# Attention with normalised q and k, then a SiLU feed-forward: squares on ScalarE, softmax sums on VectorE alone, weight rounding later and split one piece ahead

## The chip, the cores and the metric

The kernel runs on one core of one Trainium2 chip. The metric is the device time of one execution, in microseconds (us). Five queues work at once and meet only through semaphores: TensorE (PE; its weight loads are PEld), VectorE (DVE), ScalarE (ACT), GpSimd (POOL) and SyncE (SP), which here issues nearly all transfers. Each runs its own instructions strictly in order.

## What is computed

Eight batches, 12 heads, 448 positions, head size 64. Every row of q and k is divided by its root mean square and scaled by a gain; then softmax attention; then a feed-forward block of 768 -> 2048 -> 768 with SiLU over all 3584 rows.

```python
def rmsnorm(x, g):
    rms = np.sqrt(np.mean(x * x, axis=-1, keepdims=True) + 1e-06)
    return x / rms * g
scores = scale * np.matmul(q_n, k_n.transpose(0, 1, 3, 2))
attn = np.exp(scores - np.max(scores, axis=-1, keepdims=True))
attn = attn / (np.sum(attn, axis=-1, keepdims=True) + 1e-09)
x = np.matmul(attn, v)          # heads side by side: 3584 x 768
h = x @ w_in                    # 768 x 2048
return ((h * (1.0 / (1.0 + np.exp(-h)))) @ w_out).astype(np.float32)
```

The activations arrive as float32; the two weight matrices arrive as float64, and the kernel rounds them to float32 itself.

## The kernel before

**Pairs.** The work is cut into 48 *pairs*: one batch and two neighbouring heads (six pairs a batch, numbered 0 to 47 here). A row of 448 positions is folded into 112 partitions x 4 columns (`j`). For each pair the function `bounded` does: `normalise` (squares `sq`, sums per row `rms`, a power of -1/2, and the scaled rows `qn` and `kn`), `transpose` of q and of k through TensorE into `qT` and `kT`, `scores` (in two halves of two `j` each, TensorE, then the exponential `e` on ScalarE), `weigh` (`e` times `v`, into `av`), `add_up` (the softmax denominators: the sum `es` of the four `e`), `unload` (ScalarE copies `av` out as `xU`), and `divide` (a matmul with ones spreads the sums over partitions, VectorE takes the reciprocal `r` and multiplies, giving `xT`). `divide` of pair n stands inside pair n+1; `normalise` is two pairs ahead.

**Feed-forward as filler.** From pair 6 on, the feed-forward of the batch before is cut into pieces of single matmuls, and `fill()`, called four times in each pair, issues an equal share of them between the attention steps. Each block of six matmuls (`h`, line 386) is turned into `g_own` and `g_joint` by SiLU on ScalarE; the `mm` buffers that hold `h` are two, so TensorE can be one block ahead of ScalarE and no more. The second product (line 402) is evacuated by VectorE into `o` and stored. Batch 0 has no filler: its six pairs, called the *startup* below, run attention alone.

**Weights.** `w_in` comes in 24 pieces of 128 x 512, `w_out` in 32 pieces of 128 x 384. `round` makes float32 of a float64 piece: two ScalarE instructions read the low and the high words (lines 119 and 120, into `last` and into the weight itself), three VectorE instructions build the rounded bits (lines 121, 124, 128), and one GpSimd add (line 132) finishes. For `w_in` there are ten places for raw pieces and four for `last`; for `w_out` two for `last` and three for raw, the latter shared with the output tiles `o`. How many pieces are rounded in each quarter of a pair is written out by hand:

```python
rounds = [1, 0, 1, 0] if b == 0 else [3, 3, 3, 3]
```

so twelve pieces are rounded in the startup and the other 44 in pairs 6 to 9, here called the *weights stage*. Loads of raw pieces stand in SP's queue, up to ten pieces ahead, among the loads of q, k and v for two pairs ahead.

The whole order is the order of the code (manual schedule). The steps named in the prediction are at lines 274 to 292 (normalise), 306 and 308 (`qT`, `kT`), 346 and 351 (`es`), 356 (`xU`), 365 to 371 (divide), 119 to 132 (a round), 435 (the list above).

Of the kernel before, what the change touches and what calls it, by code (L numbers as in the profile page):

```python
# [46 lines left out]
class Weights:  # L47
# [7 lines left out]
    def __init__(self, nc, pool, w_in, w_out, z):  # L55
# [15 lines left out]
        self.pieces += [  # L71
            (self.W2[:, f, ts(half, z.HALF)], w_out[ts(f, P), ts(half, z.HALF)])
            for f in range(z.NF)
            for half in range(2)
        ]
        self.raws = []
        self.rounded = 0

    def load(self):
        i = len(self.raws)  # L80
        if i == len(self.pieces):
            return
        dst, src = self.pieces[i]
        raw = None
        if src.dtype == I64:
            if i < self.n_in:
                raw = self.stage[i % self.NRAW]
            else:
                raw = self.raw_pool.tile([128, 2 * dst.shape[-1]], I32, name="raw", tag="o")
            self.nc.sync.dma_start(raw.bitcast(I64), src)  # L90
        else:
            self.nc.sync.dma_start(dst, src)
        self.raws.append(raw)

    def round(self, ahead):
# [7 lines left out]
        if i == len(self.pieces):  # L103
            return
        while len(self.raws) <= i:
            self.load()
        self.rounded += 1
        if self.raws[i] is not None:
            nc = self.nc
            w = self.pieces[i][0]  # L110
            n = w.shape[-1]
            wi = w.bitcast(I32)
            words = self.raws[i].rearrange("p (n two) -> p n two", two=2)
            low, high = words[:, :, 0], words[:, :, 1]
            if i < self.n_in:
                last = self.low[i % 4]
            else:
                last = self.raw_pool.tile([128, n], I32, name="last", tag="last", bufs=2)
            nc.scalar.activation(last, low.bitcast(U32), AF.Copy, scale=2.0**-29)
            nc.scalar.activation(w, high.bitcast(F32), AF.Abs)  # L120
            nc.vector.tensor_scalar(  # L121
# [9 lines left out]
            )  # L131
            nc.gpsimd.tensor_tensor(out=wi, in0=wi, in1=last, op=ALU.add)  # L132
        while len(self.raws) < min(i + 1 + ahead, len(self.pieces)):

            if len(self.raws) >= self.n_in and self.rounded < self.n_in:
                break
            self.load()


@with_exitstack  # L140
def kernel(
# [21 lines left out]
    nc = tc.nc  # L163
# [58 lines left out]
    def arm():  # L222

        own = [dict(st) for st in state]
        w = copy.copy(weights)
        w.raws = list(weights.raws)
        return dict(
# [25 lines left out]
def bounded(  # L253
# [6 lines left out]
    mp = ctx.enter_context(tc.tile_pool(name="mp", bufs=1))  # L260
    op = weights.raw_pool = ctx.enter_context(tc.tile_pool(name="op", bufs=3))
    ps = ctx.enter_context(tc.tile_pool(name="ps", bufs=1, space=bass.MemoryType.PSUM))
# [3 lines left out]
    def normalise(n):  # L266
# [5 lines left out]
        for i, name in enumerate("qk"):  # L272
            sq = at.tile([R, 2, J, D], F32, name="sq")
            nc.gpsimd.tensor_tensor(out=sq, in0=st[name], in1=st[name], op=ALU.mult)  # L274
            nc.vector.tensor_reduce(out=rms[:, i], in_=sq, axis=AX.X, op=ALU.add)  # L275
        flat = rms.rearrange("p i h j -> p (i h j)")
# [6 lines left out]
        for i, name in enumerate("qk"):  # L283
            rows = at.tile([R, J, 2, D], F32, name=name + "n")
            st[name + "n"] = rows
            factor = rms[:, i].rearrange("p h (j one) -> p h j one", one=1)
            nc.gpsimd.tensor_tensor(
                out=rows.rearrange("p j h d -> p h j d"),
                in0=st[name],
                in1=factor.to_broadcast([R, 2, J, D]),  # L290
                op=ALU.mult,
            )

    def transpose(n, name):
# [10 lines left out]
        if name == "q":  # L305
            nc.vector.tensor_copy(dst, t)  # L306
        else:
            nc.vector.tensor_scalar_mul(out=dst, in0=t, scalar1=gains)  # L308
# [29 lines left out]
    def add_up(n, half):  # L338

        st = state[n]  # L340
        if half == 0:
            st["es"] = [at.tile([R, S], F32, name="es", bufs=2) for _ in range(2)]
        for h, eng in ((0, nc.vector), (1, nc.gpsimd)):
            es = st["es"][h]
            if half == 0:
                eng.tensor_tensor(  # L346
                    out=es, in0=st["e", 0][:, h, :], in1=st["e", 1][:, h, :], op=ALU.add
                )
            else:
                for j in (2, 3):  # L350
                    eng.tensor_tensor(out=es, in0=es, in1=st["e", j][:, h, :], op=ALU.add)  # L351

    def unload(n):
        st = state[n]
        st["xU"] = at.tile([P, S], F32, name="xU", bufs=2)
        nc.scalar.copy(st["xU"], st["av"])  # L356

    def divide(n):
# [5 lines left out]
        for h in range(2):  # L364
            nc.tensor.matmul(  # L365
                t[ds(h * D, D), :], ones[0:R, :], st["es"][h], start=True, stop=True
            )
# [9 lines left out]
    def feed_forward(b):  # L377
# [282 lines left out]
```

## Time and profile before

| | |
|---|---|
| median of 3 runs | 1708.61 us (1708.14 to 1709.46) |
| the profiled execution | 1709.11 us, span of its instructions 1707.3 us |
| PE busy | 1609.5 us, 94% of the span; mean granted clock 0.973 |
| DVE, ACT, POOL busy | 577.3, 438.9 and 583.5 us (34%, 26%, 34%) |
| transfers | 70.23 MB, 41 GB/s over the span |

The span is cut by what TensorE does: up to the first scores at 18.93 us loads and the first normalisation; then the startup, six pairs up to 124.9 us; then the weights stage, until about 300 us; then, until the last division at 1546.8 us, attention and feed-forward interleaved; then the last batch's feed-forward alone. "Granted clock" is the share of TensorE's full 2.4 GHz that it was allowed; half of that (1.2 GHz) is the other level, so a mean between 0.5 and 1 is a mixture. A row's idle time is that of its engine just before it, and the name behind the arrow is what ended it.

### The profile page before, as it was taken

Reading aid. Unit: us, or ns where it says so; the run is one execution under the profiler, and the core shown is the slowest. Engines: PE = TensorE matmul, PEld = TensorE weight load, DVE = VectorE, ACT = ScalarE, POOL = GpSimd, SP = SyncE. Lnnn points to the kernel's source line nnn. Section 1 sums busy time; section 2 is a strip of 40 time slices with the busy share of each in tenths; the row PEclk is TensorE's granted clock in tenths of the full one; section 3 lists DMA queues with packets and bytes.
Section 4 is the critical chain, followed back from the end, with each engine's and each line's share of the span. In section 5 each row is a group of like instructions: output and inputs, shape, how many; then the busy total and the mean of one; then the engine's idle time right before and its main releaser. Section 6 shows DMA issues by size and latency. Waiting matters only on the chain.

```text
span 1707.3 us, 14310 instructions
## 1 busy us (share of the span) xinstructions
PE 1609.5 (94%) x5440; PEld 792.0 (46%) x5440; DVE 577.3 (34%) x708; ACT 438.9 (26%) x696; POOL 583.5 (34%) x448
## 2 busy tenths in 40 slices
PE   4668688999999999999999999999999999999998
PEld 1223234544455444544455444554455544455555
DVE  4778766232223323232222322333222322230000
ACT  2335354123311143123311134203310133310100
POOL 6776545333323333342232333333323333310000
PEclk9878888999999999999999999999999999999999
DMA  6331343110011100110001100011001100000000
GB/s 212 94 101 62 100 126 90 51 42 17 17 31 31 42 27 6 46 41 22 17 26 31 46 17 17 26 47 32 17 11 33 54 28 17 10 10 9 1 19 20
DMA packets 51985, 70.23 MB, mean 41 GB/s; under 512 B 5316, under 2 KB 44740, under 8 KB 51908
## 3 DMA queue, kind: packets, MB, share of 16 engines
q1 hardware_dynamic: 51584, 69.23, 14.0%
q8 instruction: 45, 0.74, 0.2%
q14 instruction: 32, 0.26, 0.0%
q10 hardware_dynamic: 324, 0.00, 0.0%
HBM read 58.20 MB, written 11.01 MB: 41 GB/s over the span
## 4 chain that ended last, share of the span: by engine, by line
PE 87%; DVE 8%; POOL 2%; ACT 2%; issue 1%; DMA 0%; SPq 0%; POOLq 0%; ACTq 0%; DVEq 0%
PE mm L402 35%; PE mm L386 32%; PE sc L316 9%; PE av L330 7%; PE tr L365 2%; PE tr L302 2%; DVE W L124 1%; DVE W L128 1%; DVE es L351 1%; DVE r L369 1%; DVE W L121 1%; POOL rms L280 1%; DVE es L346 0%; POOL sq L274 0%; POOL W L132 0%
## 5 line engine op out<-in xcount | busy, mean ns | idle before, releaser
L386 PE MATMUL mm<-xT,W 128*128 128x448 f32 x1536 | 606.4, 549 | 38.1 <-ACT g_joint L394 31.7
L402 PE MATMUL mm<-W,g_own 128*128 128x384 f32 x1536 | 512.7, 489 | 0.0
L386 PEld LDWEIGHTS mm<-xT,W 128*128 128x128 f32 x1536 | 286.4, 191 | 340.2 <-issue 296.1
L402 PEld LDWEIGHTS mm<-W,g_own 128*128 128x128 f32 x1536 | 286.5, 190 | 217.9 <-issue 32.0
L321 ACT ACTIVATE e<-sc 112x896 f32<-112x896 f32 x192 | 166.5, 914 | 505.9 <-PE sc L316 395.2
L369 DVE RECIPROCAL r<-tr 128x448 f32<-128x448 f32 x48 | 141.9, 2956 | 285.8 <-PE tr L365 285.8
L274 POOL TENSOR_TENSOR sq<-k 112x512 f32<-112x512 f32 x48 | 49.9, 1039 | 468.3 <-DVE rms L275 468.3
L316 PE MATMUL sc<-qT,kT 64*112 64x448 f32 x768 | 182.1, 595 | 24.4 <-DVE kT L308 24.4
L330 PE MATMUL av<-e,v 112*64 112x448 f32 x768 | 168.6, 561 | 0.9 <-ACT e L321 0.9
L351 POOL TENSOR_TENSOR es<-es,e 112x448 f32<-112x448 f32 x96 | 128.0, 1333 | 88.9 <-ACT e L321 84.7
L280 POOL TENSOR_TENSOR rms<-rms,minus_half 112x16 f32<-112x16 f32 x48 | 139.7, 2910 | 48.4 <-DVE rms L277 48.4
L408 DVE COPY o<-mm 128x384 f32<-128x384 f32 x56 | 31.2, 557 | 341.9 <-PE mm L402 341.9
L346 POOL TENSOR_TENSOR es<-e 112x448 f32<-112x448 f32 x48 | 56.6, 1180 | 252.2 <-PE tr L365 249.1
L394 ACT ACTIVATE g_own<-mm 128x384 f32<-128x384 f32 x128 | 62.6, 489 | 280.3 <-PE mm L386 279.5
L316 PEld LDWEIGHTS sc<-qT,kT 64*112 64x112 f32 x768 | 64.6, 183 | 127.3 <-issue 85.8
L308 DVE TENSOR_SCALAR kT<-tr,gains 128x448 f32<-128x448 f32 x48 | 32.7, 682 | 197.9 <-PE tr L302 197.9
L275 DVE TENSOR_REDUCE rms<-sq 112x8 f32<-112x512 f32 x96 | 65.4, 682 | 73.9 <-POOL sq L274 73.9
L330 PEld LDWEIGHTS av<-e,v 112*64 112x64 f32 x768 | 52.2, 141 | 81.1 <-issue 66.5
L356 ACT COPY xU<-av 128x448 f32<-128x448 f32 x48 | 25.5, 532 | 237.2 <-PE av L330 237.0
L306 DVE COPY qT<-tr 128x448 f32<-128x448 f32 x48 | 29.8, 622 | 167.3 <-PE tr L302 167.3
L402 PE MATMUL mm<-W,g_joint 128*128 128x384 f32 x256 | 85.6, 490 | 0.0
L321 ACT ACT_TABLE_LOAD x44 | 56.5, 1283 | 106.0 <-PE sc L316 58.8
(38 smaller groups left out, 868.6 us busy)
## 6 DMA issues: line engine op xcount, KB each, us to landing
W<-in_moe_w_in_dram SPq DMA_DIRECT2D x24, 512.0 KB, 4.2
raw<-in_moe_w_out_dram SPq DMA_DIRECT2D x32, 384.0 KB, 3.3
q<-in_q_dram SPq DMA_DIRECT2D x48, 224.0 KB, 3.1
k<-in_k_dram SPq DMA_DIRECT2D x48, 224.0 KB, 3.6
v<-in_v_dram SPq DMA_DIRECT2D x48, 224.0 KB, 3.3
out_dram<-o SPq DMA_DIRECT2D x16, 168.0 KB, 2.1
out_dram<-o SPq DMA_DIRECT2D x16, 144.0 KB, 2.0
out_dram<-o SPq DMA_DIRECT2D x16, 120.0 KB, 2.0
```

What stands on the lines that cost most here:

```text
L274: nc.gpsimd.tensor_tensor(out=sq, in0=st[name], in1=st[name], op=ALU.mult)
L275: nc.vector.tensor_reduce(out=rms[:, i], in_=sq, axis=AX.X, op=ALU.add)
L280: nc.gpsimd.tensor_tensor(out=flat, in0=flat, in1=minus_half[0:R].to_broadcast([R, 4 * J]), op=ALU.pow)
L316: nc.tensor.matmul(banks[:, h, 0:S], st["kT"][r, ts(j, R)], st["qT"][r, :], start=True, stop=True,)
L321: nc.scalar.activation(st["e", j], banks[:, :, 0:S], AF.Exp)
L330: nc.tensor.matmul(st["av"][ds(h * D, D), :], st["v"][:, h, j, :], st["e", j][:, h, :], start=(j == 0), stop=(j == J - 1),)
L346: eng.tensor_tensor(out=es, in0=st["e", 0][:, h, :], in1=st["e", 1][:, h, :], op=ALU.add)
L351: eng.tensor_tensor(out=es, in0=es, in1=st["e", j][:, h, :], op=ALU.add)
L369: nc.vector.reciprocal(out=r, in_=t)
L386: nc.tensor.matmul(h, W1[:, c, ts(f, P)], xT[b][c], start=(c == 0), stop=(c == z.NW - 1))
L394: nc.scalar.activation(dst, h[:, cols], AF.Silu)
L402: nc.tensor.matmul(t, g[:, f, :], W2[:, f, ts(half, z.HALF)], start=(f == 0), stop=(f == z.NF - 1),)
```

## The change

1. **Squares.** `sq` on GpSimd and its buffer are gone. ScalarE writes the squares into the tiles `qn` and `kn`, which `normalise` later overwrites with the scaled rows; VectorE sums from there. So a square now waits until the transposes of the pair before have read those tiles.
2. **`qT`** is copied out by ScalarE instead of VectorE.
3. **`es`** is one tile for both heads, added by VectorE in three instructions of 112 x 896; before, VectorE did one head and GpSimd the other, three instructions of 112 x 448 each. `es` and `xU` now have one buffer per use, `o` two.
4. **Rounding** is cut in two: `split` issues the two ScalarE instructions, `round` the rest, and `round` ends by splitting the next piece. The counts per quarter become `[0, 0, 0, 1]` and `[2, 3, 2, 3]`: six pieces in the startup, 50 in pairs 6 to 10. Raw pieces of `w_out` have three buffers of their own.
5. **`w_out` by halves.** Its pieces are ordered first by column half, and the second product does all row tiles of one half before the other.

```diff
         self.pieces += [
             (self.W2[:, f, ts(half, z.HALF)], w_out[ts(f, P), ts(half, z.HALF)])
+            for half in range(2)
             for f in range(z.NF)
-            for half in range(2)
         ]
+        self.lasts = []
...
-                raw = self.raw_pool.tile([128, 2 * dst.shape[-1]], I32, name="raw", tag="o")
+                raw = self.raw_pool.tile([128, 2 * dst.shape[-1]], I32, name="raw", tag="raw", bufs=3)
...
+    def split(self):
+        i = len(self.lasts)
+        if i == len(self.pieces):
+            return
+        while len(self.raws) <= i:
+            self.load()
+        last = None
+        if self.raws[i] is not None:
+            w = self.pieces[i][0]
+            words = self.raws[i].rearrange("p (n two) -> p n two", two=2)
+            if i < self.n_in:
+                last = self.low[i % len(self.low)]
+            else:
+                last = self.raw_pool.tile([128, w.shape[-1]], I32, name="last", tag="last", bufs=2)
+            self.nc.scalar.activation(last, words[:, :, 0].bitcast(U32), AF.Copy, scale=2.0**-29)
+            self.nc.scalar.activation(w, words[:, :, 1].bitcast(F32), AF.Abs)
+        self.lasts.append(last)
...
-        while len(self.raws) <= i:
-            self.load()
+        while len(self.lasts) <= i:
+            self.split()
...
-            nc.scalar.activation(last, low.bitcast(U32), AF.Copy, scale=2.0**-29)
-            nc.scalar.activation(w, high.bitcast(F32), AF.Abs)
...
-            nc.gpsimd.tensor_tensor(out=wi, in0=wi, in1=last, op=ALU.add)
+            nc.gpsimd.tensor_tensor(out=wi, in0=wi, in1=self.lasts[i], op=ALU.add)
...
+        if len(self.lasts) < len(self.raws) and len(self.lasts) == self.rounded:
+            self.split()
...
-            sq = at.tile([R, 2, J, D], F32, name="sq")
-            nc.gpsimd.tensor_tensor(out=sq, in0=st[name], in1=st[name], op=ALU.mult)
-            nc.vector.tensor_reduce(out=rms[:, i], in_=sq, axis=AX.X, op=ALU.add)
+            rows = at.tile([R, J, 2, D], F32, name=name + "n")
+            st[name + "n"] = rows
+            by_head = rows.rearrange("p j h d -> p h j d")
+            nc.scalar.activation(by_head, st[name], AF.Square)
+            nc.vector.tensor_reduce(out=rms[:, i], in_=by_head, axis=AX.X, op=ALU.add)
...
-            nc.vector.tensor_copy(dst, t)
+            nc.scalar.copy(dst, t)
...
-        for h, eng in ((0, nc.vector), (1, nc.gpsimd)):
-            es = st["es"][h]
-            if half == 0:
-                eng.tensor_tensor(
-                    out=es, in0=st["e", 0][:, h, :], in1=st["e", 1][:, h, :], op=ALU.add
+            st["es"] = at.tile([R, 2, S], F32, name="es")
+            nc.vector.tensor_tensor(
+                out=st["es"], in0=st["e", 0], in1=st["e", 1], op=ALU.add
+            )
+        else:
+            for j in (2, 3):
+                nc.vector.tensor_tensor(
+                    out=st["es"], in0=st["es"], in1=st["e", j], op=ALU.add
...
-        for g, c0 in tiles:
-            for half in range(2):
+        for half in range(2):
+            for g, c0 in tiles:
...
-        rounds = [1, 0, 1, 0] if b == 0 else [3, 3, 3, 3]
+        rounds = [0, 0, 0, 1] if b == 0 else [2, 3, 2, 3]
```

**How the order moves, first place: VectorE in one startup pair.** VectorE's queue in the startup repeats from pair to pair. Before, one repetition reads (`W_81` is `w_in`'s float32 tile, `W_82` the room in which its raw pieces lie):

```order
L121 TENSOR_SCALAR W_81<-W_81 128x512
L124 TENSOR_SCALAR W_81<-W_81 128x512
L128 SCALAR_TENSOR_TENSOR W_81<-W_82,W_81 128x512
L369 RECIPROCAL r<-tr 128x448
L371 TENSOR_TENSOR xT<-xU,r 128x448
L346 TENSOR_TENSOR es<-e 112x448
L306 COPY qT<-tr 128x448
L351 TENSOR_TENSOR es<-es,e 112x448 x2
L121 TENSOR_SCALAR W_81<-W_81 128x512
L124 TENSOR_SCALAR W_81<-W_81 128x512
L128 SCALAR_TENSOR_TENSOR W_81<-W_82,W_81 128x512
L308 TENSOR_SCALAR kT<-tr,gains 128x448
```

Now the same stretch of VectorE's queue, from one `kT` to the next, reads:

```order
L323 TENSOR_SCALAR kT<-tr,gains 128x448
L292 TENSOR_REDUCE rms<-qn 112x8
L292 TENSOR_REDUCE rms<-kn 112x8
L294 TENSOR_SCALAR rms<-rms 112x16
L134 TENSOR_SCALAR W_81<-W_81 128x512
L137 TENSOR_SCALAR W_81<-W_81 128x512
L141 SCALAR_TENSOR_TENSOR W_81<-W_82,W_81 128x512
L383 RECIPROCAL r<-tr 128x448
L385 TENSOR_TENSOR xT<-xU,r 128x448
L358 TENSOR_TENSOR es<-e 112x896
L363 TENSOR_TENSOR es<-es,e 112x896 x2
```

The round between the last `es` and `kT` is gone, `qT` is gone, and the `es` additions are twice as wide.

**Second place: ScalarE in one startup pair.** Before, ScalarE's queue from one pair's second half to the next pair's reads:

```order
L321 ACTIVATE e<-sc 112x896 x2
L356 COPY xU<-av 128x448
L119 ACTIVATE W_82<-W_82 128x512
L120 ACTIVATE W_81<-W_82 128x512
L321 ACTIVATE e<-sc 112x896 x2
L119 ACTIVATE W_82<-W_82 128x512
L120 ACTIVATE W_81<-W_82 128x512
```

Now one repetition of it reads:

```order
L336 ACTIVATE e<-sc 112x896 x4
L321 COPY qT<-tr 128x448
L370 COPY xU<-av 128x448
L291 ACTIVATE qn<-q_58 112x2x4x64
L291 ACTIVATE kn<-k_60 112x2x4x64
L112 ACTIVATE W_82<-W_82 128x512
L113 ACTIVATE W_81<-W_82 128x512
```

The four exponentials of a pair stand together, and the copy, the two squares and the one split stand between them and the next pair's.

**Third place: ScalarE in the weights stage, at the end of pair 8.** Before, the end of a pair in that stage (pair 7) reads on ScalarE (`last` and `raw` are numbered buffers of `w_out`'s pieces, `W2_82` its float32 tile):

```order
L119 ACTIVATE last_1109<-raw_904 128x384
L120 ACTIVATE W2_82<-raw_904 128x384
L119 ACTIVATE last_1118<-raw_937 128x384
L120 ACTIVATE W2_82<-raw_937 128x384
L119 ACTIVATE last_1127<-raw_946 128x384
L120 ACTIVATE W2_82<-raw_946 128x384
L394 ACTIVATE g_own_788<-mm_1083 128x384
L394 ACTIVATE g_joint_789<-mm_1083 128x64
L394 ACTIVATE g_own_788<-mm_1139 128x384
L394 ACTIVATE g_joint_789<-mm_1139 128x64
L321 ACT_TABLE_LOAD
```

Now ScalarE's queue at the end of pair 8 reads:

```order
L291 ACTIVATE qn_1166<-q0_58 112x2x4x64
L291 ACTIVATE kn_1169<-k0_60 112x2x4x64
L112 ACTIVATE last_1182<-raw_983 128x384
L113 ACTIVATE W2_82<-raw_983 128x384
L112 ACTIVATE last_1191<-raw_992 128x384
L113 ACTIVATE W2_82<-raw_992 128x384
L112 ACTIVATE last_1200<-raw_1028 128x384
L113 ACTIVATE W2_82<-raw_1028 128x384
L408 ACTIVATE g_own_703<-mm_1151 128x384
L408 ACTIVATE g_joint_704<-mm_1151 128x64
L408 ACTIVATE g_own_703<-mm_1205 128x384
L408 ACTIVATE g_joint_704<-mm_1205 128x64
```

The two squares now stand ahead of the splits, and the splits are those of one piece later; the SiLU instructions still stand behind all of them. In SP's queue the loads of q, k and v stand behind up to twelve loads of raw `w_out` pieces, before and after.

## Rows read from the trace of the kernel before

**Rows 1.** busy time by stage: us, busy (x instructions) per engine, granted clock, DMA share, GB/s

```profile
18.93:124.90 105.97, 68.73 (x261) 24.29 (x261) 79.21 (x94) 39.22 (x55) 81.24 (x59) 0.81 0.36 107
124.90:300.00 175.10, 137.03 (x418) 62.20 (x420) 124.21 (x176) 86.81 (x154) 96.30 (x80) 0.86 0.34 97
300.00:1546.80 1246.80, 1246.80 (x4309) 619.35 (x4306) 361.72 (x419) 303.15 (x455) 397.07 (x297) 1.00 0.10 28
```

**Rows 2.** timeline of VectorE, four divisions: start, us, engine, line, operation, idle before

```profile
139.06 2.95 DVE L369 RECIPROCAL r<-tr 128x448 f32<-128x448 f32 x1
...
366.53 2.96 DVE L369 RECIPROCAL r<-tr 128x448 f32<-128x448 f32 x1 [2.07 <-PE tr L365]
...
573.98 2.96 DVE L369 RECIPROCAL r<-tr 128x448 f32<-128x448 f32 x1 [2.07 <-PE tr L365]
...
760.78 2.96 DVE L369 RECIPROCAL r<-tr 128x448 f32<-128x448 f32 x1 [2.07 <-PE tr L365]
```

**Rows 3.** chain of waits over one startup pair: start, us, what

```profile
71.12 3.35 PE sc L316 x8
...
74.63 0.92 ACT e L321
...
77.61 0.69 DVE W L128
78.30 2.88 DVE r L369
...
81.20 1.25 DVE xT L371
...
85.51 1.36 DVE es L351
...
88.39 0.61 DVE kT L308
89.05 3.35 PE sc L316 x8
```

**Rows 4.** instructions by line and shape: busy us, mean ns, idle before

```profile
L356 ACT COPY xU<-av 128x448 f32<-128x448 f32 x48 | 25.5, 532 | 237.2 <-PE av L330 237.0
...
L280 POOL TENSOR_TENSOR rms<-rms,minus_half 112x16 f32<-112x16 f32 x48 | 139.7, 2910 | 48.4 <-DVE rms L277 48.4
...
L275 DVE TENSOR_REDUCE rms<-sq 112x8 f32<-112x512 f32 x96 | 65.4, 682 | 73.9 <-POOL sq L274 73.9
```

**Rows 5.** timeline, six instructions with VectorE beside GpSimd or alone

```profile
44.79 1.26 POOL L132 TENSOR_TENSOR W<-W,W 128x512 int32<-128x512 int32 x1
...
45.33 1.21 DVE L371 TENSOR_TENSOR xT<-xU,r 128x448 f32<-128x448 f32 x1
...
76.69 0.43 DVE L121 TENSOR_SCALAR W<-W 128x512 f32<-128x512 f32 x1 [1.05 <-ACT W L120]
...
78.15 1.76 PE L316 MATMUL sc<-qT,kT 64*112 64x448 f32 x8
...
142.04 0.63 DVE L371 TENSOR_TENSOR xT<-xU,r 128x448 f32<-128x448 f32 x1
...
142.59 0.62 DVE L346 TENSOR_TENSOR es<-e 112x448 f32<-112x448 f32 x1
```

**Rows 6.** timeline around one stall of TensorE in the weights stage

```profile
202.31 0.42 SPq L183 DMA_DIRECT2D q<-in_q_dram  x1
...
202.67 0.55 PE L302 MATMUL tr<-ident,kn 112*128 112x112 f32 x4
...
207.25 1.04 POOL L274 TENSOR_TENSOR sq<-q 112x512 f32<-112x512 f32 x1
...
216.15 1.94 POOL L132 TENSOR_TENSOR W<-W,last 128x384 int32<-128x384 int32 x2
...
217.17 0.55 ACT L119 ACTIVATE last<-raw 128x384 int32<-128x384 uint32 x1 [6.96 <-POOL W L132]
...
218.69 1.11 PE L386 MATMUL mm<-xT,W 128*128 128x448 f32 x1 [9.33 <-ACT g_joint L394]
```

More of the change, by code (lines that the diff above doesn't have):

```diff
@@ L110, in round @@
             w = self.pieces[i][0]
-            n = w.shape[-1]
             wi = w.bitcast(I32)
[L113 to L118, printed above, removed]
-            nc.scalar.activation(last, low.bitcast(U32), AF.Copy, scale=2.0**-29)
-            nc.scalar.activation(w, high.bitcast(F32), AF.Abs)
+            high = self.raws[i].rearrange("p (n two) -> p n two", two=2)[:, :, 1]
             nc.vector.tensor_scalar(
@@ L225, in arm @@
         w = copy.copy(weights)
-        w.raws = list(weights.raws)
+        w.raws, w.lasts = list(weights.raws), list(weights.lasts)
         return dict(
@@ L260, in bounded @@
     mp = ctx.enter_context(tc.tile_pool(name="mp", bufs=1))
-    op = weights.raw_pool = ctx.enter_context(tc.tile_pool(name="op", bufs=3))
+    op = weights.raw_pool = ctx.enter_context(tc.tile_pool(name="op", bufs=2))
     ps = ctx.enter_context(tc.tile_pool(name="ps", bufs=1, space=bass.MemoryType.PSUM))
@@ L283, in normalise @@
         for i, name in enumerate("qk"):
-            rows = at.tile([R, J, 2, D], F32, name=name + "n")
-            st[name + "n"] = rows
             factor = rms[:, i].rearrange("p h (j one) -> p h j one", one=1)
             nc.gpsimd.tensor_tensor(
-                out=rows.rearrange("p j h d -> p h j d"),
+                out=st[name + "n"].rearrange("p j h d -> p h j d"),
                 in0=st[name],
@@ L341, in add_up @@
         if half == 0:
-            st["es"] = [at.tile([R, S], F32, name="es", bufs=2) for _ in range(2)]
-        for h, eng in ((0, nc.vector), (1, nc.gpsimd)):
-            es = st["es"][h]
-            if half == 0:
-                eng.tensor_tensor(
-                    out=es, in0=st["e", 0][:, h, :], in1=st["e", 1][:, h, :], op=ALU.add
-                )
-            else:
-                for j in (2, 3):
-                    eng.tensor_tensor(out=es, in0=es, in1=st["e", j][:, h, :], op=ALU.add)
+            st["es"] = at.tile([R, 2, S], F32, name="es")
[6 more added lines that the diff above has]
+                    out=st["es"], in0=st["es"], in1=st["e", j], op=ALU.add
+                )
     def unload(n):
         st = state[n]
-        st["xU"] = at.tile([P, S], F32, name="xU", bufs=2)
+        st["xU"] = at.tile([P, S], F32, name="xU")
         nc.scalar.copy(st["xU"], st["av"])
@@ L365, in divide @@
             nc.tensor.matmul(
-                t[ds(h * D, D), :], ones[0:R, :], st["es"][h], start=True, stop=True
+                t[ds(h * D, D), :], ones[0:R, :], st["es"][:, h, :], start=True, stop=True
             )
```

## The prediction

> **What bounds the kernel now.** I read the busy times by stage first. The reader is to see three stages [rows 1]: in the startup (18.93 to 124.90 us) TensorE is busy 68.73 of 105.97 us at a mean granted clock of 0.81; in the weights stage (to 300) 137.03 of 175.10 at 0.86; after that 1246.80 of 1246.80 at 1.00. So nothing outside the first 300 us can be gained except at the very end, which the change does not touch. The second view is the timeline of VectorE's divisions, used as a ruler [rows 2]. From the division of pair 5 to that of pair 11, the feed-forward of batch 0 passes: 366.53 - 139.06 = 227.47 us. The same work for batch 2, with no weights to round, takes 760.78 - 573.98 = 186.80. The weights stage thus wastes 40.7 us, idle time and half-clock time together. Third, the chain of waits over one startup pair [rows 3]: scores at 71.12, the next pair's at 89.05, period 17.93 us, and nearly all of it runs through VectorE: a round, `r`, `xT`, `es`, a round, `kT`. Last, a timeline around one TensorE stall in the weights stage [rows 6]: 9.33 us idle, because SiLU stood on ScalarE behind `last`, `last` behind a GpSimd add, and that add behind the whole normalisation on GpSimd (`sq` at 207.25, the add at 216.15).
>
> **The startup after the change.** I replay VectorE's queue from one `kT` to the next, time 0 at `kT`'s end.
> - Two sums of squares at 0.68 and the small factor at 0.17 [rows 4], the latter an estimate from its place between them and the round: to 1.6. The squares come from ScalarE, right after `xU`; a square is 512 elements, the copy of 448 costs 0.53 [rows 4], so I take 0.6.
> - One round, 1.6 (from 76.69 to `r` at 78.30 [rows 3, 5]): to 3.2. Its two ScalarE instructions were issued a pair earlier.
> - `r`, 2.9 [rows 3]: to 6.1. TensorE's divide is there in time: scores take 1.76 at full clock and 3.35 at half [rows 3, 5], and the divide about 1.1 more.
> - Meanwhile GpSimd: the power starts at about 1.9 and takes 2.91 [rows 4], `qn` and `kn` 1.04 each (the shape of `sq` [rows 6]), the add 1.26 [rows 5]: to 8.2.
> - `xT` is ready to go at 6.1, but the trace shows that it will not run: with GpSimd's add at 44.79 to 46.05 beside it, `xT` took 1.21 and ended 0.5 after the add; alone it takes 0.63 [rows 5]. So it ends at 8.7.
> - `es`: 448 elements take 0.62 alone [rows 5] and 1.36 beside GpSimd [rows 3]; GpSimd has nothing left in this part of the pair. For 896 I take 1.1, three times: to 12.0. (Bounds for one: 1.0, and 2.7 if blocked as in rows 3.)
> - `kT` 0.6: 12.6 us, against 17.93.
>
> The Trainium skill, SBUF — State Buffer, "Who interferes with whom", says that an instruction of VectorE with two SBUF inputs and one of GpSimd exclude each other for their whole length. The rows agree (1.21 against 0.63); without that rule the pair would come to 11.2.
>
> What hides the rest: the exponentials, transposes and `qT` (now on ScalarE, 0.53 as for `xU`) lie beside VectorE. ScalarE's four exponentials at 0.92, two copies, two squares and one split (1.1: the exponential ends at 75.55, VectorE's round starts at 76.69 [rows 3, 5]) sum to 7.0 of 12.6. The new wait is the square of k, which needs the transposes of k; behind it stand the split and the next pair's exponentials. It costs the first exponential about 0.9, and `xT`'s wait for GpSimd covers that.
>
> Sum: six pairs took 105.97, so the first took 105.97 - 5 x 17.93 = 16.3. After: the first, without divide and rounds, 11; five of 12.6; 1.3 for the one pair with two splits before its exponentials: 75.3. The exponentials' table is now loaded for the squares, ahead of need, and the first scores come 0.4 earlier. Scores of pair 6 then start near 93.8. Pair 5's division stood 14.2 after them; now two rounds instead of three are ahead of it, the second delayed by GpSimd until 9.5, so 11. It moves from 139.06 to 104.8: gain 34.3.
>
> **The weights stage after the change.** 50 rounds in five pairs instead of 44 in less than four. A round takes VectorE about 1.9 there (124.21 busy [rows 1], less some 10 of its own for each of four pairs, over 44 rounds; 1.6 is the bound below), so ten rounds and the 10 are 29 of the 31.1 that TensorE needs for a pair (186.80 / 6); GpSimd loses `sq` and `es`. So no engine is the bound, but waits in ScalarE's queue are.
> - Pair 6: TensorE reaches the matmul that needs pair 5's `xT` at 11.2 after the scores, and has it at 14.7: 3.5, with 1.5 for the half clock behind it: 5.
> - Pairs 7 and 8, last quarter: the third `last` has to wait for the add two pieces before, and that add stands behind the normalisation on GpSimd, as today. Counted from the end of the transposes of k (203.2 in rows 6): square and sum 1.5, factor and start 0.5, power 2.9, two multiplies 2.1, two adds 2.2, one split 1.1, SiLU 0.7, semaphores 0.6: 11.6. TensorE has 6.1 of work meanwhile (203.2 to 218.69 - 9.33 = 209.36), so it idles 5.5 where it idled 9.33. Half clock afterwards adds 2.5 (scores 3.35 for 1.76 and a few matmuls). 8 each: 16.
> - Pairs 9 and 10 have no SiLU behind the splits; only the next exponentials come late, under a quarter of filler: 2 in all.
>
> Waste 23 instead of 40.7: gain 17.7.
>
> **At nothing.** `w_out` by halves changes no matmul and no store's size; the first half is rounded before it is needed. Two `o` buffers instead of three still let one be filled while the other is stored. From 300 us on, ScalarE is busy 303 of 1247 us [rows 1]; two squares and a copy a pair add 1.73 x 37 = 64, hidden under TensorE's continuous work, and 64 is the price if none of it were.
>
> **Sum.** The profiled execution took 1709.1 (span 1707.3 and 1.8 around it). 1709.1 - 34.3 - 17.7 = 1657.1. The median of the runs is 0.5 below that execution: 1656.6. Own range 1645 to 1672.
>
> **Rivals.**
> - *The clock stays low in the startup.* For: mean 0.81 there, and the scores ran at 3.35, half speed, after every wait for `kT` [rows 1, 3]. Then scores, `weigh` and transposes at half clock make TensorE the loop: 16 a pair. Against: TensorE idles 6.2 us a pair now (105.97 less 68.73, over six) and would idle 1 to 3. Loss against mine 5 x 3.4 = 17: 1674. The Trainium skill, TensorE: Matmul & The Clock Gate, "Part 1: The HAM clock gate (the "warmup" mystery)", says that the throttled state is the default and activity releases it; by that a loop with TensorE busy three quarters of the time should do better than now, but no run here shows it.
> - *Waste goes with the pairs that round.* 40.7 over 3.67 pairs is 11.1 a pair; five pairs make 55.5. For: the same chain `last`, add, power stands there. Against: GpSimd has 2 x 1.04 less in it, and the stall's length is 6.1 less than the chain's. 1709.1 - 34.3 + 14.8 - 0.5 = 1689.
> - *No stall is left:* the early split takes SiLU off the chain, waste 5: 1639.
> - *Slower: q arrives late and ScalarE stands for it.* In SP's queue q for two pairs ahead stands behind up to twelve raw pieces that wait for rounds; at 202.31 it was issued only 4.9 before its use on GpSimd [rows 6]. Now its reader is ScalarE, with SiLU and all exponentials behind it. Lateness adds one for one to the stall. With 5 more than today's per pair, 16 to 19 in five pairs make 80 to 95: the startup gain of 34.3 is gone from 15 a pair upward (75 = 40.7 + 34.3). At 19: 1709.1 - 34.3 + 54.3 - 0.5 = 1729. Against: raws are loaded three deep, and 6.1 us of filler follow the round that frees the last of them.
> - *The startup doesn't shorten,* because GpSimd's power and the squares' path (square, sum, power, two multiplies: 8 in a row) set its pace: 1709.1 - 17.7 - 0.5 = 1691; with the waste unchanged too, 1709, no change.
>
> **How the numbers follow.** Mine 0.56; low clock 0.14; waste with pairs 0.12; no stall 0.09; slower 0.05; startup not shorter 0.04. Range 1638 to 1689 holds all but about 0.15. A measurement here tells about 0.2%, 3.4 us, from no change: faster 0.92, same 0.03, slower 0.05.
>
> **What would show it.** Startup scores 12 to 13 apart in place of 17.93, `es` of 112 x 896 near 1.1, `xT` near 2 or waiting for GpSimd, pair 5's division near 105; from there to pair 11's about 210 instead of 227; two idles of TensorE of 5 to 6 us ended by SiLU, in pairs 7 and 8; nothing idle after pair 11. I am wrong if the startup's period stays above 15, if squares wait for q's transfer, or if any wait of TensorE shows up after 350 us.

## The result and the profile after

The changed kernel takes 1668.22 us (median of 4 runs, 1666.87 to 1669.05) against 1708.38 (1708.07 to 1709.46): ratio 0.9763, 95% interval 0.9746 to 0.978. The forecast was 1656.6 with a range of 1638 to 1689: the direction was right and the time lay in the range, but 11.6 us of the forecast gain of 52 did not come. The profiled execution has a span of 1666.6 us and a mean granted clock of 0.986.

The busy times by stage answer to [rows 1]; the columns are the same.

```profile
18.43:110.00 91.57, 73.99 (x310) 27.66 (x311) 78.84 (x90) 52.23 (x80) 48.85 (x31) 0.91 0.43 122
110.00:300.00 190.00, 162.37 (x518) 76.68 (x518) 125.17 (x184) 95.15 (x169) 79.52 (x62) 0.92 0.36 103
...
350.00:1500.00 1150.00, 1150.00 (x3965) 570.29 (x3964) 327.20 (x349) 342.93 (x533) 165.41 (x102) 1.00 0.10 27
```

TensorE is still continuously busy from 350 us on, though ScalarE does two squares and a copy more in each pair. All of the difference lies before that. The ruler of VectorE's divisions ([rows 2]) says where; here are the divisions of pairs 5 to 11.

```profile
100.61 2.94 DVE L383 RECIPROCAL r<-tr 128x448 f32<-128x448 f32 x1
...
134.69 2.96 DVE L383 RECIPROCAL r<-tr 128x448 f32<-128x448 f32 x1 [0.51 <-PE tr L379]
...
175.79 2.96 DVE L383 RECIPROCAL r<-tr 128x448 f32<-128x448 f32 x1 [3.86 <-PE tr L379]
...
220.34 2.96 DVE L383 RECIPROCAL r<-tr 128x448 f32<-128x448 f32 x1 [3.79 <-PE tr L379]
...
257.42 2.95 DVE L383 RECIPROCAL r<-tr 128x448 f32<-128x448 f32 x1
...
299.75 2.96 DVE L383 RECIPROCAL r<-tr 128x448 f32<-128x448 f32 x1 [5.54 <-PE tr L379]
...
325.79 2.96 DVE L383 RECIPROCAL r<-tr 128x448 f32<-128x448 f32 x1 [2.05 <-PE tr L379]
```

Pair 5's division moved from 139.06 to 100.61: 38.45 us, where 34.3 were forecast. From there to pair 11's it takes 225.18 instead of 227.47: a gain of 2.29, where 17.7 were forecast. The two make 40.7, the whole of the difference between the profiled executions (spans 1707.3 and 1666.6). So the startup paid more than forecast, and the weights stage next to nothing. Cut at the first scores of pair 6 instead (124.90 before, 93.8 forecast, 90.87 after), the gains are 34.0 and 6.7 us where 31.1 and 20.9 were forecast: the sizes depend on the cut, the finding does not.

The ruler can be read pair by pair. Each interval between two divisions, less the interval of the same two pairs in batch 2 (32.88, 32.12, 32.12, 31.61, 32.04 and 26.04, 186.81 together), is the waste of that pair in us. In pair 6 the ruler shows less than was lost when pair 5's division comes late, since TensorE has then worked ahead of it:

| pair | 6 | 7 | 8 | 9 | 10 | 11 | sum |
|---|---|---|---|---|---|---|---|
| before | 13.5 | 13.7 | 13.6 | -0.1 | 0.0 | 0.0 | 40.7 |
| forecast | 5 | 8 | 8 | 2 for both | | 0 | 23 |
| after | 1.2 | 9.0 | 12.4 | 5.5 | 10.3 | 0.0 | 38.4 |

What TensorE waited for in that stage, as a table of its waits (engine and line waited for: us in total, times, longest):

```profile
PE mm L400 <- ACT g_joint L408: 18.4, 3, 9.9
PE mm L416 <- POOL W L145: 6.9, 2, 6.3
PE mm L400 <- DVE xT L385: 3.7, 1, 3.7
PE mm L416 <- DVE o L422: 2.3, 1, 2.3
```

And ScalarE's own waits there, from the same view:

```profile
ACT last L112 <- POOL W L145: 40.6, 11, 8.3
...
ACT qn L291 <- DMA q<-in_q_dram: 14.3, 3, 6.1
```

The first line is the chain that the prediction named: `last` behind GpSimd's adds, and these behind the normalisation. The second is the wait that it held unlikely: a square waits for the transfer of q, three times. The timeline of pair 8 shows both, ending in TensorE's longest stall (start, us, engine, line, operation, idle before):

```profile
181.73 10.63 SPq L91 DMA_DIRECT2D raw<-in_moe_w_out_dram  x5
...
192.41 0.42 SPq L198 DMA_DIRECT2D q<-in_q_dram  x1
...
192.49 0.55 PE L317 MATMUL tr<-ident,kn 112*128 112x112 f32 x4
...
196.37 0.63 ACT L291 ACTIVATE qn<-q 112x512 f32<-112x512 f32 x1 [3.68 <-DMA q<-in_q_dram]
...
198.95 2.94 POOL L297 TENSOR_TENSOR rms<-rms,minus_half 112x16 f32<-112x16 f32 x1 [5.84 <-DVE rms L294]
...
203.97 1.94 POOL L145 TENSOR_TENSOR W<-W,last 128x384 int32<-128x384 int32 x2
204.99 0.55 ACT L112 ACTIVATE last<-raw 128x384 int32<-128x384 uint32 x1 [6.18 <-POOL W L145]
...
207.48 1.86 PE L400 MATMUL mm<-xT,W 128*128 128x448 f32 x2 [9.92 <-ACT g_joint L408]
```

Read it from the top. SyncE issues five raw loads over 10.63 us, since each waits until a round frees its buffer; q's load stands behind them in the same queue and is issued at 192.41. The square of q starts at 196.37, 3.68 us after ScalarE was free for it; the transposes of k, which the square of k behind it needs, had ended at 193.04. On GpSimd the power, two multiplies and two adds follow one after the other; when the first of the adds ends `last` gets its buffer, then SiLU runs, then TensorE. It is the stall of [rows 6], 9.92 where that was 9.33. Before, q was issued at the same point of the pair (202.31, the transposes of k at 202.67), but GpSimd came to its square only at 207.25, behind other work and without a wait: the load is no later than it was, its reader is earlier.

### The profile page after: what moved, and what is told of

Read it like the earlier page. It is cut to its first block, busy times and chain, and to the rows that moved or that the text cites. A ratio compares the mean times of both kernels' runs of the same rounds, so it can differ in the third digit from the quotient of the medians.

```text
span 1666.6 us, 14205 instructions
## 1 busy us (share of the span) xinstructions
PE 1599.6 (96%) x5440; PEld 789.0 (47%) x5440; DVE 561.4 (34%) x660; ACT 516.9 (31%) x840; POOL 307.0 (18%) x208
## 4 chain that ended last, share of the span: by engine, by line
PE 83%; DVE 2%; issue 1%; POOL 1%; ACT 1%; POOLq 0%
PE mm L416 33%; PE mm L400 32%; PE sc L331 8%; PE av L345 7%; PE tr L379 2%; PE tr L317 2%; POOL W L145 0%; DVE r L383 0%; DVE W L141 0%; DVE es L363 0%; DVE W L137 0%; DVE W L134 0%; ACT W L113 0%; ACT last L112 0%; DVE es L358 0%
## 5 line engine op out<-in xcount | busy, mean ns | idle before, releaser
L416 PE MATMUL mm<-W,g_own 128*128 128x384 f32 x1536 | 517.9, 493 | 9.3 <-POOL W L145 6.9
L331 PE MATMUL sc<-qT,kT 64*112 64x448 f32 x768 | 175.4, 577 | 13.9 <-DVE kT L323 13.9
L363 DVE TENSOR_TENSOR es<-es,e 112x896 f32<-112x896 f32 x96 | 108.7, 1133 | 11.4 <-ACT e L336 2.9
L291 ACT ACTIVATE kn<-k 112x512 f32<-112x512 f32 x48 | 30.2, 630 | 166.5 <-issue 155.6
L321 ACT COPY qT<-tr 128x448 f32<-128x448 f32 x48 | 25.6, 533 | 146.1 <-PE tr L317 146.1
L336 ACT ACT_TABLE_LOAD x43 | 55.2, 1283 | 35.5 <-PE sc L331 34.8
L416 PEld LDWEIGHTS mm<-W,g_joint 128*128 128x128 f32 x256 | 47.7, 190 | 37.3 <-issue 7.6
L408 ACT ACT_TABLE_LOAD x44 | 56.5, 1283 | 0.8
L358 DVE TENSOR_TENSOR es<-e 112x896 f32<-112x896 f32 x48 | 54.2, 1129 | 3.0 <-ACT e L336 3.0
```

What stands on the lines that cost most here:

```text
L331: nc.tensor.matmul(banks[:, h, 0:S], st["kT"][r, ts(j, R)], st["qT"][r, :], start=True, stop=True,)
L336: nc.scalar.activation(st["e", j], banks[:, :, 0:S], AF.Exp)
L358: nc.vector.tensor_tensor(out=st["es"], in0=st["e", 0], in1=st["e", 1], op=ALU.add)
L363: nc.vector.tensor_tensor(out=st["es"], in0=st["es"], in1=st["e", j], op=ALU.add)
L408: nc.scalar.activation(dst, h[:, cols], AF.Silu)
L416: nc.tensor.matmul(t, g[:, f, :], W2[:, f, ts(half, z.HALF)], start=(f == 0), stop=(f == z.NF - 1),)
```

## The experiments

The theory for the 11.6 us: in the weights stage two chains meet in ScalarE's in-order queue, q's late transfer in front of the squares (new) and the last quarter's splits behind the normalisation (old). Rival: the waste goes with the number of pieces rounded in these pairs, whatever the order. Each run was compared with the kernel before on the same chip (median there 1707.3 to 1707.9); ratios are to it. Differences to the changed kernel are between chips, and the medians of the kernel before differ by up to 1.1 us between these.

**q's loads no longer behind raw loads.** A round asks for raw pieces ten ahead, though `w_out` has three raw buffers; here it asks for two ahead.

```diff
     def round(self, ahead):
...
+        if self.rounded >= self.n_in:
+            ahead = 2
```

> The changed kernel, with raw w_out pieces loaded two ahead instead of ten, so that q, k and v for two pairs ahead no longer stand behind raw pieces that wait for rounds. Theory A (late q is part of the waste in the weights stage): the squares' three waits for q's transfer (3.7, 4.5 and 6.1 us in pairs 8, 9 and 10) go, TensorE's idles of 9.9, 2.3 and 6.3 us shrink to about 6, 0 and 2, the time falls by 8 to 12 us to 1656 to 1660. Rival B (the waste goes with the amount of rounding, whatever waits for what): the waits go, the time stays at 1668 within 2.

Measured: 1653.03 us (1651.57 to 1654.18), ratio 0.9674 (0.9658 to 0.969): 15.2 below the changed kernel, better than expected; 13.9 of it lies in the weights stage. No square waits for q any more, and the idles of 9.92, 2.34 and 6.31 shrink to 6.20, nothing and 1.67, as expected; that of pair 7 stays (7.06). The waste by pair becomes 2.8, 9.3, 9.1, 1.5 and 1.9 (24.5 in all): pairs 8, 9 and 10 give back 3.4, 4.0 and 8.4. The next load of q (199.42) stands behind two raw loads that take 1.59 (197.78); in pair 8 the stall of 6.20, ended by SiLU, is left (205.07). TensorE's waits in the stage:

```profile
PE mm L402 <- ACT g_joint L410: 15.6, 3, 7.1
PE mm L418 <- POOL W L145: 2.5, 2, 1.7
...
```

The waits for GpSimd's adds in the second product went from 6.9 to 2.5 and that for `o` is gone, so they hung on these loads too. The edit also brings forward the loads of k and v and the stores in the same queue, so the 15.2 need not be q's alone.

**The last quarter's rounds ahead of the normalisation.**

```diff
-        normalise(n + 2)
         for _ in range(rounds[3]):
             weights.round(weights.NRAW)
+        normalise(n + 2)
```

> The changed kernel with the last quarter's rounds ahead of normalise instead of behind it, so that GpSimd's adds stand before power and multiplies. Theory A: ScalarE's third split no longer waits for the normalisation, TensorE's idles in pairs 7, 8 and 10 (7.0, 9.9, 6.3 us) fall to under 2 each although q still comes late, the time falls by 18 to 25 us to 1643 to 1650. Rival B: VectorE's and ScalarE's load is unchanged, so the time stays within 4 of 1668, other waits taking their place. A loss of up to 0.5 us per startup pair (3 us) is possible in both, since the power starts a round later.

Measured: 1643.99 us (1642.52 to 1645.08), ratio 0.9626 (0.961 to 0.9642): 24.2 below the changed kernel, a time inside the expected range. The idles were not as expected: under 2 us each was expected, and TensorE still waits 4.50 us for SiLU in pair 7 and 4.22 in pair 8. The waste is 18.1 (0.9, 7.8, 6.9, 1.0, 1.5). The adds that `last` waits for no longer stand behind power and multiplies, but they wait for VectorE's rounds now, and `last` for up to 8.1 us for them. The squares stand behind the splits, and none of them waits for q any more (in pair 8 q is issued at 185.14 and squared at 192.89), so this run takes away the new chain along with part of the old one. The new wait is that of TensorE's transposes for `qn` (7.1 in five waits, all in the startup), as the normalisation comes later. The startup became faster all the same, which the theory had not counted on: its divisions are 11.93 apart (pairs 0 to 4), where the changed kernel has 12.53 on the mean (82.94 - 32.81 over four), and pair 6's first scores come at 89.05 instead of 90.87. The timeline of VectorE and GpSimd in one such pair:

```profile
42.89 1.28 POOL L145 TENSOR_TENSOR W<-W,W 128x512 int32<-128x512 int32 x1 [4.34 <-DVE W L141]
...
44.12 2.95 DVE L383 RECIPROCAL r<-tr 128x448 f32<-128x448 f32 x1
...
47.10 0.63 DVE L385 TENSOR_TENSOR xT<-xU,r 128x448 f32<-128x448 f32 x1
...
47.64 1.93 DVE L358 TENSOR_TENSOR es<-e 112x896 f32<-112x896 f32 x1
48.59 1.89 POOL L302 TENSOR_TENSOR kn<-k,rms 112x512 f32<-112x512 f32 x1
```

The add runs before the division; `xT` takes 0.63 without it, and `es` and `kn` are the ones that delay each other.

**Both together.**

```diff
+        if self.rounded >= self.n_in:
+            ahead = 2
...
-        normalise(n + 2)
         for _ in range(rounds[3]):
             weights.round(weights.NRAW)
+        normalise(n + 2)
```

> Both: raw pieces two ahead, and the last quarter's rounds ahead of normalise. Theory A: no idle of TensorE over 2 us between pair 7 and pair 10, waste of the weights stage about 10 (the wait for pair 5's xT, 3.7, stays), time 1638 to 1646. Rival B: 1664 to 1670.

Measured: 1640.9 us (1636.24 to 1641.51), ratio 0.9598 (0.9582 to 0.9615). The time is in the expected range, but that no idle above 2 us would be left was wrong: TensorE idles 4.51 in pair 7 and 3.24 in pair 8, and the waste is 14.7, nearly all in these pairs (7.6 and 6.4). In pair 7 ScalarE's `last` still waits 8.07 for a GpSimd add. The two edits share 12.1 us of their gain (15.2 and 24.2 apart, 27.3 together); with either of them no square waits for q any more. What is left in pair 7 is the third split of the last quarter, which waits for a buffer of `last`.

**A third buffer of `last`,** on top of these (a small constant tile was laid into an existing one to make room).

```diff
-                last = self.raw_pool.tile([128, w.shape[-1]], I32, name="last", tag="last", bufs=2)
+                last = self.raw_pool.tile([128, w.shape[-1]], I32, name="last", tag="last", bufs=3)
```

> Raw pieces two ahead, the last quarter's rounds ahead of normalise, and three buffers for the low words of w_out instead of two. Theory A: the idles of TensorE that are left (4.5 and 3.2 us in pairs 7 and 8, ended by SiLU behind a split that waits for GpSimd's add) shrink by 1.5 to 3 each, with their half clock; the time 1633 to 1639 against 1640.9. Rival B (VectorE's pace of the rounds is what SiLU waits for): 1640 within 2.

Measured: 1632.42 us (1630.63 to 1633.38), ratio 0.9556 (0.954 to 0.9572), 0.6 below the expected range, 35.8 below the changed kernel. The waste is 6.1; of TensorE's waits in the stage this is left:

```profile
PE mm L402 <- ACT g_joint L410: 5.4, 2, 3.3
```

The idle of pair 7 is gone; that of pair 8, which was expected to shrink too, is 3.31 where it was 3.24. Its beginning is another now: the split in front of SiLU waits 2.34 for the transfer of its raw piece (185.36). In the whole stage the splits wait 33.2 us for raw pieces, so asking only two ahead has a price as well.

These four runs round the same 50 pieces in the same quarters and have wastes of 24.5, 18.1, 14.7 and 6.1. The rival, waste by the amount of rounding whatever the order, is refuted.

**Other counts on top of that.**

```diff
-        rounds = [0, 0, 0, 1] if b == 0 else [2, 3, 2, 3]
+        rounds = [0, 0, 0, 1] if b == 0 else [3, 2, 3, 2]
```

> The best version so far (splits and raw loads ahead, last rounds before the normalisation, three buffers of last; 1632.4) with the counts [3, 2, 3, 2] in place of [2, 3, 2, 3] per quarter. Theory A (what is left is SiLU behind the splits of the last quarter; with two there instead of three it goes): the 3.3 us idle of TensorE in pair 8 goes, 1629 to 1632. Rival (the first quarter then holds three rounds ahead of the division on VectorE, which makes xT later for the first product of the quarter after it): an idle of TensorE ended by xT or r appears, 1632 to 1637.

Measured: 1632.6 us (1631.04 to 1634.38), ratio 0.9555 (0.9539 to 0.9571): no change, and the rival was right on the cause. The SiLU waits fell to 1.9, and in their place the three rounds of the first quarter make the division of pair 5, and so `xT`, late:

```profile
PE mm L402 <- DVE xT L387: 4.4, 1, 4.4
...
```

**The parts of the change, undone one at a time on the changed kernel.** First the counts of rounds.

```diff
-        rounds = [0, 0, 0, 1] if b == 0 else [2, 3, 2, 3]
+        rounds = [1, 0, 1, 0] if b == 0 else [3, 3, 3, 3]
```

> The changed kernel with the old counts of rounds: twelve in the startup, 44 in pairs 6 to 9. If the moved engines' work made the startup short, its period is near 14 (one round of 1.6 more on VectorE than 12.3) and pair 5's division near 115; the waste of the weights stage stays near 40 (theory A: the same chain in as many quarters) and the time is 1680 to 1686. If it was the deferred rounding, the period is near 16 to 17.9 and the time 1695 to 1705.

Measured: 1675.85 us (1675.02 to 1676.58), ratio 0.9812 (0.9795 to 0.9828): only 7.6 above the changed kernel, less than expected. Pair 5's division comes at 113.86, 13.3 later, but the stage then wastes 31.7 instead of 38.4, 6.7 less. Fewer rounds in the startup paid, and half was given back.

Then `w_out`'s column halves as well (pieces and second product in the old order), on top of the old counts, since with the new ones the first tile would need pieces that are not rounded yet.

```diff
-            for half in range(2)
             for f in range(z.NF)
+            for half in range(2)
...
-        for half in range(2):
-            for g, c0 in tiles:
+        for g, c0 in tiles:
+            for half in range(2):
```

> The changed kernel with the old counts of rounds (as in the run with old counts, 1675.85) and in addition w_out ordered as before the change: pieces by row block, both halves in turn, and the second product tile by tile. It prices the column halves by difference with that run. Theory A (the halves are worth nothing where twelve pieces a pair are rounded, since all of w_out is there when the second product needs it): 1674 to 1679. Rival (the first tiles wait for pieces of the other half that the order by halves had put later): 3 to 10 us more, 1679 to 1686, with TensorE waiting for GpSimd's adds in pairs 9 and 10.

Measured: 1674.47 us (1673.9 to 1675.64), ratio 0.9805 (0.9789 to 0.9821). Against 1675.85 that is no difference beyond the intervals: with twelve pieces a pair the halves are worth nothing. What they are worth with the new counts was not tried.

Then the squares back on GpSimd, into the same tiles.

```diff
-            nc.scalar.activation(by_head, st[name], AF.Square)
+            nc.gpsimd.tensor_tensor(out=by_head, in0=st[name], in1=st[name], op=ALU.mult)
```

> The changed kernel with the squares computed by GpSimd (into the same tiles), everything else as changed. Theory A (in the startup VectorE's queue sets the pace, and GpSimd's adds delay xT in it): two squares of 1.04 put GpSimd's power, multiplies and add some 1 to 2 us later, so a startup pair takes 13.3 to 14 in place of 12.3, pair 5's division moves from 100.6 to 106 to 110, the time to 1673 to 1680. Rival B (who squares doesn't matter, only the rounds and the sums do): 1668 within 2.

Measured: 1685.14 us (1684.22 to 1686.38), ratio 0.9867 (0.9851 to 0.9884): 16.9 above the changed kernel, more than expected. A startup pair takes 13.59, and the stage wastes 47.7. The timeline of one pair shows why the startup lost more than GpSimd's own time:

```profile
51.70 1.97 POOL L291 TENSOR_TENSOR qn<-q 112x512 f32<-112x512 f32 x1 [0.42 <-PE tr L317]
...
52.87 3.59 DVE L363 TENSOR_TENSOR es<-es,e 112x896 f32<-112x896 f32 x2
```

The squares fall beside `es`, and each delays the other: two `es` take 3.59 instead of 2.29, and the GpSimd squares 1.97 and 1.62 (51.70, 53.88) where the same shape took 1.04 in [rows 6]. This is not the old arrangement: before, `sq` had a tile of its own, while these squares wait for the transposes that read `qn` and `kn`. So 16.9 is the price of the engine with the tiles as changed.

Then the softmax sums shared again, head 0 on VectorE and head 1 on GpSimd.

```diff
+        for h, eng in ((0, nc.vector), (1, nc.gpsimd)):
+            es = st["es"][:, h, :]
...
+                    eng.tensor_tensor(out=es, in0=es, in1=st["e", j][:, h, :], op=ALU.add)
```

> The changed kernel with the softmax sums shared again: head 0 on VectorE, head 1 on GpSimd, 112x448 each. Theory A (the two engines exclude each other in additions): each of VectorE's three takes 1.4 instead of 0.6, 4.2 a pair against 3.3 for the three wide ones, and GpSimd's following work starts later; a startup pair takes 13.3 to 14.5, pair 5's division 106 to 112, the time 1674 to 1684. Rival B (halving VectorE's elements wins): a startup pair 11 to 12, the time 1662 to 1668.

Measured: 1673.22 us (1672.74 to 1675.66), ratio 0.98 (0.9783 to 0.9816): 5.0 above, just under the expected range; pair 5's division comes at 103.41, earlier than the 106 expected.

```profile
60.98 1.53 POOL L361 TENSOR_TENSOR es<-e 112x448 f32<-112x448 f32 x1
...
61.43 1.56 DVE L361 TENSOR_TENSOR es<-e 112x448 f32<-112x448 f32 x1
...
63.10 2.85 DVE L366 TENSOR_TENSOR es<-es,e 112x448 f32<-112x448 f32 x2
```

VectorE needs 1.56 + 2.85 = 4.41 us for half the sums with GpSimd beside it, and in the changed kernel's startup 1.08 + 2.29 = 3.37 for all of them alone: the helper costs more than it takes off. (In two of five startup pairs there, where a GpSimd add lies beside the first sum, all of them take 4.45.)

Last, `qT` back on VectorE.

```diff
-            nc.scalar.copy(dst, t)
+            nc.vector.tensor_copy(dst, t)
```

> The changed kernel with qT copied out by VectorE again. Theory A: 0.6 more on VectorE's queue in each startup pair, 12.9 in place of 12.3, and TensorE's transposes of k wait a little longer for it; the time 1670 to 1673. Rival B (VectorE waits for TensorE there anyway): 1668 within 1.5.

Measured: 1673.17 us (1672.85 to 1674.97), ratio 0.9796 (0.9779 to 0.9812): 5.0 above, at the edge of the expected range. Pair 4's division is as early as in the changed kernel (83.02 against 82.94); the loss is in pair 5 (2.1) and in the weights stage (42.6 against 38.4). So the expected cause, 0.6 more in each startup pair, did not show, though the time came out near; why it costs where it does stays open.

Counts 7.6, squares 16.9, sums 5.0 and `qT` 5.0 make 34.5, where the whole change gained 40.2 us. These are losses on undoing one part with the others in place; parts that lean on each other are counted twice or not at all, as the two edits above show, so 5.7 is no price of the split and the raw buffers. Those were not run apart.

## Why the prediction was right and where it failed

**Startup: right, by its mechanism.** The forecast period was 12.6; first scores of successive pairs, from 29.79 to 90.87 us over five pairs, are 12.2 apart, and those of pair 6 stood at 90.87 where 93.8 was forecast. Here are these two and the replayed repetition as it ran, answering to [rows 3]:

```profile
29.79 1.76 PE L331 MATMUL sc<-qT,kT 64*112 64x448 f32 x8 [0.78 <-DVE kT L323]
...
50.01 1.08 DVE L358 TENSOR_TENSOR es<-e 112x896 f32<-112x896 f32 x1
...
51.19 2.29 DVE L363 TENSOR_TENSOR es<-es,e 112x896 f32<-112x896 f32 x2
...
51.88 0.63 ACT L291 ACTIVATE qn<-q 112x512 f32<-112x512 f32 x1
...
53.40 0.68 DVE L323 TENSOR_SCALAR kT<-tr,gains 128x448 f32<-128x448 f32 x1
...
54.13 2.42 PE L331 MATMUL sc<-qT,kT 64*112 64x448 f32 x8 [2.24 <-DVE kT L323]
...
58.30 2.96 DVE L383 RECIPROCAL r<-tr 128x448 f32<-128x448 f32 x1 [1.31 <-PE tr L379]
...
60.63 1.27 POOL L145 TENSOR_TENSOR W<-W,W 128x512 int32<-128x512 int32 x1
...
61.29 1.09 DVE L385 TENSOR_TENSOR xT<-xU,r 128x448 f32<-128x448 f32 x1
...
90.87 1.76 PE L331 MATMUL sc<-qT,kT 64*112 64x448 f32 x8 [2.07 <-DVE kT L323]
```

Each term held: square 0.63 (0.6 forecast), `es` 1.08 and 2.29 for two (1.1 each), `xT` 1.09 beside GpSimd's add and ending 0.48 after it (forecast: it ends 0.5 after). One place was off: the division waits 1.31 for TensorE, which the replay had ready in time. It cost nothing, since `xT` would have waited for GpSimd's add anyway. GpSimd's power began 1.5 us after `kT`, not 1.9, and so `xT` ended at 8.3 of the pair instead of 8.7: five times 0.4. The 1.3 us for one pair's extra split did not appear, and the second round in front of pair 5's division cost less (9.74 after the scores, 11 forecast). Together these are 4.5 us; the first pair took 0.6 longer than its 11 from a start 0.4 earlier, which leaves about the 4.2 of surplus.

The run with rounds ahead of the normalisation bears out that the add held `xT` back: with the add elsewhere `xT` takes 0.63. The pair did not fall to the 11.2 named for that (by the prediction's own terms, with `xT` ending at 6.7, it would be 10.6), but to 11.9, because `es` and `kn` collide there instead. And half the sums beside GpSimd took VectorE 4.41 us, all of them alone 3.37. The Trainium skill, SBUF — State Buffer, "Who interferes with whom", says that a VectorE instruction with two SBUF inputs contends with a GpSimd instruction that reads SBUF. Both runs agree; GpSimd's power does not follow it (last section).

**Rival of the low clock: wrong.** The mean granted clock of the startup rose from 0.81 to 0.91 with TensorE busy 73.99 of 91.57 us (81%) instead of 65%, and most scores took 1.76. The rival of a startup that does not shorten, because of GpSimd and the squares' path, is wrong with it.

**At nothing: right.** TensorE does not wait from 300 to 1500 us; SiLU, squares and copies are hidden. The exponentials' table was indeed loaded once for a square (one of 1283 ns at line 291, 43 at the exponentials instead of 44). The two `o` buffers were not quite free: one `o` waited 4.61 us for a store (278.21), in pair 10, where SP's queue issued four stores behind q's loads.

**The weights stage: the failed step.** Forecast waste 23, measured 38.4. Of the terms, pair 6 (5 forecast) was 1.2: the idle for `xT` was 3.68 as forecast (3.5), and SiLU added 1.41. But from 93.37 on TensorE had done 7.2 us of the pair's work before pair 5's division at 100.61; in batch 2 only 0.2 of it stands before the division (533.01, 533.23). So the ruler hides about 7 us of what was lost in pair 6, and the prediction, which put the division 11 after the scores and added the full idle to 186.80, had not counted this head start. That its sum came no further off is in this part luck.

Pair 7 (8 forecast) was 9.0:

```profile
154.96 3.01 POOL L297 TENSOR_TENSOR rms<-rms,minus_half 112x16 f32<-112x16 f32 x1 [0.63 <-PE mm L400]
...
158.05 1.17 POOL L302 TENSOR_TENSOR qn<-q,rms 112x512 f32<-112x512 f32 x1
158.35 3.50 DVE L141 SCALAR_TENSOR_TENSOR W<-raw,W 128x384 int32<-128x384 int32 x1
159.18 1.04 POOL L302 TENSOR_TENSOR kn<-k,rms 112x512 f32<-112x512 f32 x1
160.18 1.26 POOL L145 TENSOR_TENSOR W<-W,W 128x512 int32<-128x512 int32 x1
161.40 2.26 POOL L145 TENSOR_TENSOR W<-W,last 128x384 int32<-128x384 int32 x2
162.73 0.55 ACT L112 ACTIVATE last<-raw 128x384 int32<-128x384 uint32 x1 [8.34 <-POOL W L145]
...
164.25 1.86 PE L400 MATMUL mm<-xT,W 128*128 128x448 f32 x2 [7.04 <-ACT g_joint L408]
```

The chain has the links that the prediction counted, and the idle of 7.04 was priced at 5.5: from the end of the transposes of k (151.94) to TensorE's next product it took 12.3 instead of 11.6, and TensorE had 5.3 of work meanwhile instead of 6.1. The first link is the longer one: the power starts 3.0 after the transposes where 2.0 was counted, since VectorE does `kT` (152.81) and q's sum ahead of k's. That VectorE was held up for 3.50 did not lengthen the chain: GpSimd worked without a gap from 154.96 on.

Pairs 8 to 10 are where it went wrong: 12.4, 5.5 and 10.3 instead of 8 and "2 in all". The sentence that failed is the one against the slower rival, that raws are loaded three deep and that 6.1 us of filler follow the round that frees the last of them. The three buffers fill at once, and the rest of the up to ten pieces asked for ahead stand in SP's queue until rounds of the same pair free them; q stands behind them. The rival's condition was met: squares waited 3.68, 4.48 and 6.13 for q, which is one of the three signs by which the prediction said it would be wrong. Its price of 16 to 19 a pair was not: asking for two pieces ahead took 13.9 us off the stage, near the 15.4 that it wasted beyond the forecast, and left 9.3 and 9.1 in pairs 7 and 8 and 3.4 in the two after them, where 8, 8 and 2 were forecast. With the startup's surplus of 4.2 set against the 15.4, these are 11.2 of the 11.6 us. The second thing not foreseen is what the lateness ran into: without SiLU behind the splits, the second product itself waits, for the last adds of half 1 (pair 10, below) and for `o` behind a round (2.34 at 252.69, pair 9):

```profile
279.97 0.63 ACT L291 ACTIVATE qn<-q 112x512 f32<-112x512 f32 x1 [6.13 <-DMA q<-in_q_dram]
...
287.39 1.95 POOL L145 TENSOR_TENSOR W<-W,last 128x384 int32<-128x384 int32 x2
...
288.43 2.93 PE L416 MATMUL mm<-W,g_own 128*128 128x384 f32 x4 [6.31 <-POOL W L145]
```

The prediction looked for the reader of each late piece in the queue of ScalarE alone; here it is TensorE directly.

**Open:** the split and the raw buffers were not run alone, the old order of `w_out` not with the new counts, and q's load was not moved without the other transfers of its queue.

## What to carry to other kernels

When an operation moves to another engine, its inputs' lateness moves with it: the late q was harmless to GpSimd's queue, and freeing its queue gave 15 us when ScalarE read it, because SiLU and the splits stand behind the square. A load that asks for more buffers than there are blocks everything behind it in its queue: with three buffers ten ahead was too many, and two ahead was better, though the splits then wait for raw pieces (other distances were not tried). Work that gives buffers back (here the adds) belongs ahead of work that nobody waits for yet (here the normalisation of a pair two ahead): that one swap was worth 24 us, more than half as much as the whole change, part of it because it also hides the late q.

## What the runs showed of the hardware

VectorE and GpSimd, when both run instructions with two tensor inputs, hold each other up in both directions, and the victim may wait for several instructions: one of 0.56 us took 3.50 with three GpSimd instructions (`qn`, `kn`, an add) back to back beside it, though two of them started after it, and GpSimd's `kn` took 1.89 instead of 1.04 with `es` beside it. VectorE's instructions with one tensor input are not spared: in the changed kernel line 137, which takes 0.43 alone (139.69), took 3.37 beside `qn`, `kn` and an add (95.62). GpSimd's power, which also has two inputs but of 112 x 16, runs for 3.0 us and did not hold up the round beside it: line 141, two inputs as well, took 0.69 in the startup with the power around it. Why it is exempt no run here shows. So what counted here is not how long GpSimd was busy, but which of its instructions lay beside which of VectorE's.
